# Single-head products in 64-by-32 tiles of the matrix engine, in a packed attention with gated convolution and experts

## The chip, the cores and the metric

The program runs on one core of one Trainium2 chip. The metric is the device time of one execution in microseconds; the figure for a kernel is the median of several executions.

## What is computed

The reference has eight batches of 576 positions and three stages, all in 32-bit floating point.

```python
# q, k, v: (8 batches, 8 heads, 576, 64); p: (8, 8, 32, 64)
p_packed = softmax(p @ k.T / 8) @ v               # 32 packed rows per head
out = softmax(q @ p_packed.T / 8) @ p_packed      # back to 576 rows
x = heads side by side                            # (8, 576, 512)
gate = sigmoid(causal depthwise convolution of x with conv_w, 5 taps)
y = (gate * (x @ w_val)) @ w_out
logits = y @ w_gate; local = sigmoid(y @ w_local)
# each position takes argmax(logits), or the expert of the one before it where local >= 0.5
out = p[e] * (relu(y @ w1[e]) @ w2[e])
```

## The kernel before

**The order of the work.** The kernel is written as tasks. Each task names its engine, an estimated duration and the buffers it reads and writes; `Plan.run` (line 93) plays the program forward with these estimates and emits the tasks in the order in which they would start, the most urgent first by due times. The products of the expert (`expert`, line 828) have goals spaced over a period of 87 us per batch, and everything else is due by what depends on it. So attention of the next batch is laid between the expert products of this one on the matrix engine (PE). `SETUP` (line 186) lists the first transfers in order; those of k, v, q and the two weight matrices go through the queue of SP, and in later batches the loads go through POOL. Four buffers (`RAW`, line 18) hold k, v and q; three buffers in PSUM (`NPP`, pool `psp`) serve all products but those of the expert, which have two of their own (`NPF`).

**The heads.** The eight heads are two groups `g` of four. A group's four heads stand as two pairs. In `s1` (line 335) the operand `pb` is block-diagonal: two heads' p on 128 rows by 64 columns, with zeros in the other halves, so that one product over 128 rows gives two heads' scores in 64 partitions, and two such products side by side fill 128 partitions. Each is done for two halves of 288 positions, four products for a group. Every 32-bit product shows as two PE instructions in the trace, so a group's `s1` is 8 instructions (line 345), tile 128x64, 288 columns.

**The chain of a batch.** For each group: `s1`; its softmax (maximum on DVE line 350, exponential on ACT line 352, into one shared tile `a1`); `a1T`, five transposes (line 366); `a1v` (line 372), which multiplies the 5 blocks of 128 positions by v for two pairs, 20 instructions of 128x64 tiles with 128 columns (line 380), and on DVE scales and masks the result into a block-diagonal `ppf` (line 385); `ppT`, its transpose (line 409); `s2` (line 414), again 8 instructions (line 425) against q; and `mval` (line 504), which multiplies the packed rows by w_val, 4 instructions with 512 columns (line 510). Then come the second softmax, `xT` (line 515: the mixed values, in tiles of 64 rows by 128 columns, one instruction for each product, line 531), the convolution, `val` (the value product by M and the second softmax), `logits` (line 674: 16 instructions in tiles of 128x32, line 684), `route` and `x2`. In batch 0 the scores are first copied to a fixed tile `s2t` and transposed on PE, the taps of the convolution are spread by `taps` (line 548, ahead of all batches) and `conv0` (line 566) replaces `xT`; single products there are in plain 32 bits. Later batches use three products of split operands (`mm3`, lines 298 to 300), one instruction each.

**The first stretch.** `from_f64` (line 876) turns w_val, conv_w and w_out from 64-bit numbers to 32 bits with ACT and DVE (lines 882 to 895), w_val in two halves. `mval` of group 0 needs the first half alone.

Of the kernel before, what the change touches and what calls it, by code (L numbers as in the profile page):

```python
# [17 lines left out]
NP = 32  # L18
# [40 lines left out]
class Plan:  # L59
# [33 lines left out]
    def run(self):  # L93
# [8 lines left out]
        free = dict.fromkeys(engs, 0.0)  # L102
        lock, dma = 0.0, 0.0
# [13 lines left out]
        while todo:  # L117
# [72 lines left out]
def packed_attention_gated_conv_moe(  # L190
# [49 lines left out]
    a1 = const.tile([128, 640], F32, name="a1")  # L240
    s2t = [const.tile([128, 640], F32, name=f"s2t{i}") for i in range(2)]
# [7 lines left out]
    f = {n: Fixed() for n in ("ident", "mask", "cs", "cw", "ww", "wval", "wout", "a1", "s20", "s21", "lt",  # L249
# [69 lines left out]
    def load(b, kind, g, q):  # L319
        if kind == "p":  # L320
            t = st[b, "p"] = ref(ld, [128, 4, 128], F32, "pb", f"pb{b}", 1)
            x = dma(q, 262144, lambda: q.dma_start(t[:], pbd[b]), w=[t], behind=[] if b else done("load"))
            if not b:
                st["load"] = x
            return
# [6 lines left out]
    def pair(i):  # L332
        return slice(i * 64, i * 64 + 64)

    def s1(b, g):
        pb, kt = st[b, "p"], st[b, "k", g]
        r = st[b, "r1", g] = ref(sm, [128, 4], F32, "s1r", f"s1r_{b}_{g}", 2)
        sc = lambda: two(a1[:, 0:S])
        ps = pst([128, 2, 512], f"s1_{b}_{g}")

        def prod():
            for hf in range(2):
                for i in range(2):
                    n = slice(i * S + hf * HS, i * S + hf * HS + HS)
                    nc.tensor.matmul(ps[pair(i), hf, 0:HS], pb[:, 2 * g + i, pair(i)], kt[:, n],  # L345
                                     start=True, stop=True)

        pe(8 * 125, prod, r=[pb, kt], w=[ps], behind=done("a1T"))
# [4 lines left out]
            ps=True, r=[ps], w=[f["a1"], r])  # L353
# [7 lines left out]
    def a1T(b, g):  # L361
        ps = pst([128, 8, 128], f"a1Tp_{b}_{g}")

        def prod():
            for c in range(NT):
                nc.tensor.transpose(ps[:, c, :], a1[:, c * 128:c * 128 + 128], ident)  # L366

        st["a1T"] = pe(5 * 109, prod, r=[f["a1"], f["ident"]], w=[ps], behind=done("a1v"))
# [3 lines left out]
    def a1v(b, g):  # L372
# [4 lines left out]
        def prod():  # L377
            for c in range(NT):
                for i in range(2):
# [5 lines left out]
        dve(188, lambda: stt(pf[:], ps[:, 0:128], r[:, 3:4], mask, ALU.mult, ALU.mult),  # L385
# [20 lines left out]
    def ppT(b, g):  # L406
        pf = st[b, "pp", g][0]
        ps = pss1(f"ppTp_{b}_{g}")
        pe(110, lambda: nc.tensor.transpose(ps[:, 0:128], pf[:], ident), r=[pf, f["ident"]], w=[ps],
           behind=done((b - 1, "s2"), (b - 1, "mval")))  # L410
        t = st[b, "ppT", g] = ref(wk, [128, 128], F32, "ppT", f"ppT_{b}_{g}", 2)
        act(128, lambda: cp(t[:], ps[:, 0:128], AF.Copy), ps=True, r=[ps], w=[t])

    def s2(b, g):


        t, qt = st[b, "ppT", g], st[b, "q", g]
        sT, sk = s2t[g], f[f"s2{g}"]
        pk = pst([128, 2, 512], f"s2k_{b}_{g}")

        def prod():
            for hf in range(2):
                for i in range(2):
                    n = slice(i * S + hf * HS, i * S + hf * HS + HS)
                    nc.tensor.matmul(pk[pair(i), hf, 0:HS], t[:, pair(i)], qt[:, n], start=True, stop=True)  # L425

        st[b, "s2"] = pe(8 * 125, prod, r=[t, qt], w=[pk], behind=done((b - 1, "a2T")))
        if b:
            softmax2(b, g, pk)
            return  # L430
        act(S, lambda: cp(two(sT[:, 0:S]), halves(pk), AF.Copy), ps=True, r=[pk], w=[sk])
# [6 lines left out]
        pe(5 * 109, turn, r=[sk, f["ident"]], w=[ps])  # L438
# [65 lines left out]
    def mval(b, g):  # L504
        t = st[b, "ppT", g]
        ps = pst([128, 2, 512], f"mv_{b}_{g}")

        def prod():
            for i in range(2):
                nc.tensor.matmul(ps[pair(i), 0, :], t[:, pair(i)], wval[:, 2 * g + i, :], start=True, stop=True)  # L510

        st[b, "mval"] = pe(4 * 250, prod, r=[t, (f["wval"], g)], w=[ps], behind=done((b - 1, "val")))
        st[b, "M", g] = operand(b, f"mh{g}", f"ml{g}", ps, DM, lambda: ps[:, 0, :])
# [34 lines left out]
    def taps():  # L548
# [15 lines left out]
        pe(40 * 112, prod, r=[f["cw"], f["ident"]], w=st["taps"])  # L564
# [311 lines left out]
    def from_f64(n, dst, t, at, ct, gt, r, w, eng="DVE", later=0):  # L876
# [5 lines left out]
        act(n, lambda: cp(dst(), low().bitcast(U32), AF.Copy, scale=2.0 ** -52), r=r[:1], w=r[1:], later=later)  # L882
        act(n, lambda: cp(gt(), high().bitcast(F32), AF.Abs), r=r[:1], w=[rg], later=later)
# [260 lines left out]
```

## Time and profile before

| | |
|---|---|
| median of 3 runs | 743.12 us (741.96 to 743.38) |
| the profiled execution's own time | 742.84 us |
| its span, from the first to the last instruction | 741.2 us |
| PE busy | 709.5 us, 96% |
| DVE, ACT, POOL busy | 427.9, 288.0, 236.5 us |
| granted PE clock, mean over the span | 0.992 |

The chain of waits leads back from the last instruction to whatever released each step. The groups of instructions give the busy time of one line; PE instructions overlap there, so a line's sum is less than its count times its mean. How far one run of instructions holds PE is read from the chain, where each piece ends as the next begins.

### The profile page before, as it was taken

The numbers are of one execution on the slowest core, as the hardware profiler recorded it, in microseconds if no ns is written. First come the engines' busy times: TensorE is split into PE (matmuls) and PEld (weight loads), VectorE is DVE, ScalarE is ACT, GpSimd is POOL, SyncE is SP. The second block draws the span as 40 slices with busy tenths as digits, with TensorE's granted clock in tenths as the row PEclk, the third lists the DMA queues.
The fourth block names the chain that finished last, engine by engine and source line by source line (L and its number), as shares of the span: only waits on it lengthen the run. The fifth ranks groups of instructions, "written<-read, shape, count | busy, mean of one in ns | idle before, by whom it ended". The sixth has DMA issues, their size and how long they took to land.

```text
span 741.2 us, 13948 instructions
## 1 busy us (share of the span) xinstructions
PE 709.5 (96%) x5492; PEld 651.8 (88%) x5492; DVE 427.9 (58%) x872; ACT 288.0 (39%) x556; POOL 236.5 (32%) x250
## 2 busy tenths in 40 slices
PE   4689999999999999999989999899999999999996
PEld 2368889989979978997989979899899999999996
DVE  3983589568786878357852578427773463321310
ACT  2534455334543445423433334434343233322420
POOL 1020432244141334302443134422254035424441
PEclk9899999999999999999999999999999999999999
DMA  8611671376262366234452355424143325243421
GB/s 332 254 46 47 213 245 56 124 262 215 82 188 101 117 245 180 88 141 147 157 164 73 127 181 162 126 57 170 49 134 88 142 82 151 80 148 130 128 91 66
DMA packets 35623, 103.59 MB, mean 140 GB/s; under 512 B 4282, under 2 KB 6770, under 8 KB 32994
## 3 DMA queue, kind: packets, MB, share of 16 engines
q0 software_dynamic: 13952, 58.24, 22.5%
q1 hardware_dynamic: 21314, 44.20, 19.9%
q8 instruction: 45, 0.74, 0.4%
q10 hardware_dynamic: 288, 0.21, 0.1%
q14 instruction: 24, 0.20, 0.1%
HBM read 76.48 MB, written 28.52 MB: 142 GB/s over the span
## 4 chain that ended last, share of the span: by engine, by line
PE 88%; DVE 4%; DMA 4%; ACT 1%; issue 1%; POOL 0%; SPq 0%; ACTq 0%; POOLq 0%; DVEq 0%
PE g L298 18%; PE g L300 17%; PE g L299 17%; PE x L298 5%; PE x L299 5%; PE x L300 5%; PE pp L380 3%; PE s L345 2%; PE s2k L425 2%; PE val L299 2%; PE val L300 2%; PE val L298 2%; DMA codes<-rk 2%; PE xT L531 2%; PE mv L510 2%; PE a1Tp L366 1%
## 5 line engine op out<-in xcount | busy, mean ns | idle before, releaser
L313 POOL TENSOR_TENSOR wlo<-raw,whi 128x512 fp32r<-128x512 f32 x128 | 167.2, 1307 | 282.1 <-ACT whi L311 281.6
L298 PE MATMUL g<-x2h,whi 128*128 128x288 f32 x512 | 153.5, 300 | 6.0 <-DVE hl L845 5.7
L298 PE MATMUL g<-hh,whi 128*128 128x288 f32 x512 | 154.9, 302 | 0.0
L300 PE MATMUL g<-x2h,wlo 128*128 128x288 f32 x512 | 151.5, 296 | 0.0
L299 PE MATMUL g<-x2l,whi 128*128 128x288 f32 x512 | 151.3, 296 | 0.0
L300 PE MATMUL g<-hh,wlo 128*128 128x288 f32 x512 | 150.8, 294 | 0.0
L299 PE MATMUL g<-hl,whi 128*128 128x288 f32 x512 | 150.8, 294 | 0.0
L311 ACT ACTIVATE whi<-raw 128x512 fp32r<-128x512 f32 x128 | 80.3, 627 | 108.3 <-PE g L299 58.5
L845 DVE SCALAR_TENSOR_TENSOR hl<-g,hh 128x288 fp32r<-128x288 f32 x128 | 57.8, 454 | 93.7 <-ACT hh L843 93.2
L298 PEld LDWEIGHTS g<-x2h,whi 128*128 128x128 f32 x512 | 96.8, 189 | 10.7 <-DVE hl L845 7.2
L298 PEld LDWEIGHTS g<-hh,whi 128*128 128x128 f32 x512 | 96.2, 188 | 8.7 <-issue 8.3
L843 ACT ACTIVATE hh<-g 128x288 fp32r<-128x288 f32 x128 | 52.6, 411 | 115.7 <-PE g L300 115.5
L299 PEld LDWEIGHTS g<-x2l,whi 128*128 128x128 f32 x512 | 96.7, 189 | 0.0
L300 PEld LDWEIGHTS g<-x2h,wlo 128*128 128x128 f32 x512 | 96.6, 189 | 0.0
L299 PEld LDWEIGHTS g<-hl,whi 128*128 128x128 f32 x512 | 96.1, 188 | 0.0
L300 PEld LDWEIGHTS g<-hh,wlo 128*128 128x128 f32 x512 | 96.0, 188 | 0.0
L543 DVE SCALAR_TENSOR_TENSOR acc<-xT,cw,acc 128x572 f32<-128x572 f32 (+3 forms) x112 | 84.2, 806 | 5.9 <-ACT acc L539 5.9
L298 PE MATMUL x<-gh,wout_hi 128*128 128x288 f32 x256 | 76.0, 297 | 0.0
L299 PE MATMUL x<-gl,wout_hi 128*128 128x288 f32 x256 | 75.7, 296 | 0.0
L300 PE MATMUL x<-gh,wout_lo 128*128 128x288 f32 x256 | 75.3, 294 | 0.0
L863 DVE TENSOR_TENSOR y<-g,rows 128x288 f32<-128x288 f32 x64 | 29.0, 454 | 63.8 <-PE g L300 63.7
L641 DVE SCALAR_TENSOR_TENSOR x2l<-x,x2h 128x576 fp32r<-128x576 f32 x32 | 24.2, 757 | 68.5 <-ACT x2h L640 68.5
(171 smaller groups left out, 1093.7 us busy)
## 6 DMA issues: line engine op xcount, KB each, us to landing
raw<-in_wE_dram SPq DMA_DIRECT2D x128, 256.0 KB, 2.7
xs<-x2h POOLq DMA_DIRECT2D x8, 1152.0 KB, 4.6
xs<-x2l POOLq DMA_DIRECT2D x8, 1152.0 KB, 7.2
v<-in_v_dram POOLq DMA_DIRECT2D x14, 640.0 KB, 5.3
out_dram<-y POOLq DMA_DIRECT2D x31, 288.0 KB, 3.1
k<-in_kT_dram POOLq DMA_DIRECT2D x14, 576.0 KB, 5.3
q<-in_qT_dram POOLq DMA_DIRECT2D x14, 576.0 KB, 4.7
rows<-rk SPq DMA_DIRECT2D x8, 288.0 KB, 3.7
```

The source lines that it names most:

```text
L298: nc.tensor.matmul(o, lhi, rhi, start=start, stop=False)
L299: nc.tensor.matmul(o, lhi, rlo, start=False, stop=False)
L300: nc.tensor.matmul(o, llo, rhi, start=False, stop=stop)
L311: t = act(n, lambda: cp(hi(), src(), AF.Copy), ps=ps, r=r, w=[h], behind=behind)
L313: pool(n, lambda: nc.gpsimd.tensor_tensor(lo(), src(), f32(hi()), ALU.subtract), r=[*r, h], w=[l])
L345: nc.tensor.matmul(ps[pair(i), hf, 0:HS], pb[:, 2 * g + i, pair(i)], kt[:, n], start=True, stop=True)
L380: nc.tensor.matmul(ps[pair(i), 0:128], t[:, c, pair(i)], vt[:, c * 256 + i * 128:c * 256 + i * 128 + 128], start=(c == 0), stop=(c == NT - 1))
L543: dve(S + 60, lambda i=i, j=j, k=k, d=d, acc=acc: stt(acc[:, d:], x(i)[:, 0:S - d], cw[:, j, k:k + 1], acc[:, d:], ALU.mult, ALU.add), r=[ ...
L641: dve(S, lambda: stt(two(xlo[:, m, :]), halves(ps), 0.5, f32(two(xhi[:, m, :])), ALU.mult, ALU.subtract), r=[ps, (xhi, m)], w=[(xlo, m)])
L843: act(HS, lambda ps=ps, u=u, n=n: cp(hh[:, u, n], ps[:, 0:HS], AF.Relu), ps=True, r=[ps], w=[(hh, (u, hf))], goal=goal, urgent=True)
L845: dve(HS, lambda ps=ps, u=u, n=n: stt(hl[:, u, n], ps[:, 0:HS], 0.0, f32(hh[:, u, n]), ALU.max, ALU.subtract), r=[ps, (hh, (u, hf))], w=[( ...
L863: dve(HS, lambda ps=ps, hf=hf, n=n, y=y: tt(y[:, n], ps[hf][:, 0:HS], st[b, "w"][:, n], ALU.mult), r=[ps[hf], st[b, "w"]], w=[(y, hf)], go ...
```

## The change

Every product of a single head becomes a tile of its own of 64 rows by 32 columns. The two groups stand in the upper and lower 64 partitions (`row(g)`), the four heads of a group in four strips of 32 columns (`col(i)`). `s1`, `s2` and `mval` now do both groups in one task, eight heads in turn, and need no zeros. `a1v` keeps a task for each group, with tiles of 128 rows by 32 columns and 64 moving columns. One new ACT step writes the packed rows of both groups into `ppc`, and one transpose replaces two. The inputs are laid out on the host to fit. With them go new estimates and starting values of the planner, another order of the first transfers, a later place of `taps`, two `a1` tiles, four accumulators where there were five, and an exponential ahead of the program's work.

```diff
-        free = dict.fromkeys(engs, 0.0)
-        lock, dma = 0.0, 0.0
+        free = dict.fromkeys(engs, 900.0)
+        lock, dma = 0.0, 2200.0
...
-                dma = max(t.end, dma) + t.size / 290.0
+                dma = max(t.end, dma) + t.size / (RATE if dma < 25000 else 290.0)
...
+STEP8, STEPV = 30, 27
+TAPS, WARM, RATE, S1B = 'a1v', True, 415.0, [(0, 'xT', 1)]
...
-ACC, WLO, F64 = 5, "POOL", "DVE DVE"
-SETUP = "id k0 p v0 q0 cs cw wv0 k1 v1 wv1 q1 wo0 wo1"
+ACC, WLO, F64 = 4, "POOL", "DVE DVE"
+SETUP = "id k0 k1 p v0 cs cw wv0 v1 q0 wv1 q1 wo0 wo1"
...
-            t = st[b, "p"] = ref(ld, [128, 4, 128], F32, "pb", f"pb{b}", 1)
+            t = st[b, "p"] = ref(ld, [128, 4, NP], F32, "pb", f"pb{b}", 1)
...
+    def heads():
+        return [(i, g) for i in range(4) for g in range(2)]
+    def row(g):
+        return slice(g * 64, g * 64 + 64)
+    def col(i):
+        return slice(i * NP, i * NP + NP)
+    def s1(b):
+        pb, kt = st[b, "p"], [st[b, "k", j] for j in range(2)]
+        ps = [pst([128, 2, 512], f"s1_{b}_{g}") for g in range(2)]
+        def prod():
+            for hf in range(2):
+                for i, g in heads():
+                    n = slice(i % 2 * S + hf * HS, i % 2 * S + hf * HS + HS)
+                    nc.tensor.matmul(ps[g][col(i), hf, 0:HS], pb[row(g), i, :], kt[i // 2][row(g), n],
+                                     start=True, stop=True)
+        pe(STEP8 * 32 + 250, prod, r=[pb, *kt], w=ps, behind=done("a1T") + (done(*S1B) if b == 1 else []))
...
             for c in range(NT):
-                for i in range(2):
-                    nc.tensor.matmul(ps[pair(i), 0:128], t[:, c, pair(i)],
-                                     vt[:, c * 256 + i * 128:c * 256 + i * 128 + 128],
+                for i in range(4):
+                    nc.tensor.matmul(ps[col(i), 0:D], t[:, c, col(i)], vt[:, c * 256 + i * D:c * 256 + i * D + D],
                                      start=(c == 0), stop=(c == NT - 1))
-        st["a1v"] = pe(20 * 62, prod, r=[t, vt], w=[ps], behind=done("xT"))
+        st["a1v"] = pe(40 * STEPV + 250, prod, r=[t, vt], w=[ps], behind=done("xT"))
+        act(D + 90, lambda: cp(pc[:, g, :], ps[:, 0:D], AF.Copy, scale=r[:, 3:4]), ps=True, r=[ps, r], w=[(pc, g)])
...
+    def ppT(b):
+        pc = st[b, "ppc"]
+        pe(110, lambda: nc.tensor.transpose(ps[:, 0:128], pc.t.rearrange("p g d -> p (g d)"), ident),
...
+    def s2(b):
+        pk = [pst([128, 2, 512], f"s2k_{b}_{g}") for g in range(2)]
+                for i, g in heads():
+                    nc.tensor.matmul(pk[g][col(i), hf, 0:HS], t[row(g), col(i)], qt[i // 2][row(g), n],
+                                     start=True, stop=True)
...
+    def mval(b):
+            for i, g in heads():
+                nc.tensor.matmul(ps[col(i), g, :], t[row(g), col(i)], wval[row(g), i, :], start=True, stop=True)
+        st[b, "mval"] = pe(16 * STEP8 * 16 // 9 + 250, prod, r=[t, f["wval"]], w=[ps], behind=done((b - 1, "val")))
...
-        pe(40 * 112, prod, r=[f["cw"], f["ident"]], w=st["taps"])
+        pe(40 * 60, prod, r=[f["cw"], f["ident"]], w=st["taps"], behind=done(TAPS))
...
+        s1(b)
         for g in range(2):
-            s1(b, g)
             a1T(b, g)
             a1v(b, g)
-            ppT(b, g)
-            mval(b, g)
+        ppT(b)
+        mval(b)
+        if not b:
+            taps()
...
+        s2(b)
+        for g in range(2):
             a2T(b, g)
...
+    if WARM:
+        cp(lt[64:, 4, :], lt[64:, 4, :], AF.Exp)
```

## Rows read from the trace of the kernel before

**Rows 1.** The page, part 1: busy us of each engine, share of the span, instructions.

```profile
PE 709.5 (96%) x5492; PEld 651.8 (88%) x5492; DVE 427.9 (58%) x872; ACT 288.0 (39%) x556; POOL 236.5 (32%) x250
```

**Rows 2.** The page, part 4: the chain that ended last, by engine.

```profile
PE 88%; DVE 4%; DMA 4%; ACT 1%; issue 1%; POOL 0%; SPq 0%; ACTq 0%; POOLq 0%; DVEq 0%
```

**Rows 3.** Windows: stretch, length, busy us of PE PEld DVE ACT POOL, clock, DMA, GB/s.

```profile
0.00:20.00 20.00, 8.72 (x51) 5.27 (x52) 7.85 (x21) 6.31 (x12) 4.09 (x11) 1.00 0.88 340
20.00:40.00 20.00, 13.65 (x107) 8.28 (x107) 18.91 (x30) 10.62 (x14) 1.60 (x3) 0.83 0.58 219
40.00:65.00 25.00, 23.43 (x157) 19.00 (x157) 17.88 (x24) 11.07 (x16) 4.68 (x2) 1.00 0.06 21
```

**Rows 4.** Groups of PE instructions by line and shape, the lines that the change touches.

```profile
L380 PE MATMUL pp<-v,a1T 128*64 128x128 f32 x320 | 21.9, 286 | 0.8 <-ACT a1T L370 0.8
L345 PE MATMUL s<-k,pb 128*64 128x288 f32 x128 | 20.2, 439 | 5.7 <-DMA pb<-in_pbd_dram 5.7
L425 PE MATMUL s2k<-q,ppT 128*64 128x288 f32 x128 | 19.8, 432 | 1.0 <-ACT ppT L412 1.0
L510 PE MATMUL mv<-wval,ppT 128*64 128x512 f32 x64 | 17.4, 624 | 0.8 <-DVE wval L895 0.6 <-DVE rr L732 0.2
```

**Rows 5.** The chain in order of time: start us, us, engine, tile, line, instructions.

```profile
58.54 3.88 PE val L614 x16
...
62.42 3.47 PE wwp L667 x32
...
154.35 1.09 PE pp L380 x20
155.45 0.86 PE mv L510 x4
156.30 0.97 PE s L345 x8
...
166.63 0.98 PE xT L531 x12
167.61 1.12 PE s L345 x8
```

**Rows 6.** The chain in the window 199 to 202 us, in order of time.

```profile
199.11 1.11 PE lg L684 x16
200.22 1.24 PE pp L380 x20
201.46 0.26 PE ppTp L409
201.72 0.14 PE g L298
```

**Rows 7.** Instructions in order of time, first stretch: start us, us, engine, line.

```profile
5.74 2.19 PE L345 MATMUL s<-k,pb 128*64 128x288 f32 x8 [5.74 <-DMA pb<-in_pbd_dram]
...
7.96 0.76 DVE L350 TENSOR_REDUCE s1r<-s 128x1 f32<-128x576 f32 x1 [6.44 <-PE s L345]
...
8.99 1.28 ACT L352 ACT_TABLE_LOAD   x1 [8.99 <-DVE s1r L351]
...
22.77 2.38 PE L560 MATMUL taps<-ident,cw 128*64 128x128 f32 x40
...
29.19 1.22 DVE L895 SCALAR_TENSOR_TENSOR wval<-gt,wval 128x1024 f32<-128x1024 f32 x1
...
30.72 0.48 PE L409 MATMUL ppTp<-ident,ppf 128*128 128x128 f32 x1 [4.48 <-DVE ppf L385]
...
31.85 2.19 PE L425 MATMUL s2k<-q,ppT 128*64 128x288 f32 x8 [0.65 <-ACT ppT L412]
```

**Rows 8.** DMA issues by line: transfers, count, KB each, median us from issue to landing.

```profile
k<-in_kT_dram SPq DMA_DIRECT2D x2, 576.0 KB, 9.7
...
pb<-in_pbd_dram SPq DMA_DIRECT2D x1, 256.0 KB, 4.3
```

**Rows 9.** The page, part 5: an expert product, its busy us and the idle time before it.

```profile
L298 PE MATMUL g<-x2h,whi 128*128 128x288 f32 x512 | 153.5, 300 | 6.0 <-DVE hl L845 5.7
```

More of the change, by code (lines that the diff above doesn't have):

```diff
@@ L239, in packed_attention_gated_conv_moe @@
     wout_lo = const.tile([128, 4, DM], F32R, name="wout_lo")
-    a1 = const.tile([128, 640], F32, name="a1")
-    s2t = [const.tile([128, 640], F32, name=f"s2t{i}") for i in range(2)]
+    a1 = [const.tile([128, 640], F32, name=f"a1_{i}") for i in range(2)]
     lt = const.tile([128, NT, 9], F32, name="lt")
@@ L320, in load @@
         if kind == "p":
-            t = st[b, "p"] = ref(ld, [128, 4, 128], F32, "pb", f"pb{b}", 1)
-            x = dma(q, 262144, lambda: q.dma_start(t[:], pbd[b]), w=[t], behind=[] if b else done("load"))
+            t = st[b, "p"] = ref(ld, [128, 4, NP], F32, "pb", f"pb{b}", 1)
+            x = dma(q, 65536, lambda: q.dma_start(t[:], pbd[b]), w=[t], behind=[] if b else done("load"))
             if not b:
@@ L365, in prod @@
             for c in range(NT):
-                nc.tensor.transpose(ps[:, c, :], a1[:, c * 128:c * 128 + 128], ident)
-        st["a1T"] = pe(5 * 109, prod, r=[f["a1"], f["ident"]], w=[ps], behind=done("a1v"))
+                nc.tensor.transpose(ps[:, c, :], a1[g][:, c * 128:c * 128 + 128], ident)
+        st["a1T"] = pe(5 * 109, prod, r=[f[f"a1{g}"], f["ident"]], w=[ps], behind=done("a1v"))
         t = st[b, "a1T", g] = ref(wk, [128, NT, 128], F32, "a1T", f"a1T_{b}_{g}", 1)
@@ L404, in operand, with softmax2_0 @@
         return hi, lo
[L406 to L411, printed above, removed]
+    def ppT(b):
+        pc = st[b, "ppc"]
+        ps = pss1(f"ppTp_{b}")
+        pe(110, lambda: nc.tensor.transpose(ps[:, 0:128], pc.t.rearrange("p g d -> p (g d)"), ident),
+           r=[pc, f["ident"]], w=[ps], behind=done((b - 1, "s2"), (b - 1, "mval")))
+        t = st[b, "ppT"] = ref(wk, [128, 128], F32, "ppT", f"ppT_{b}", 2)
         act(128, lambda: cp(t[:], ps[:, 0:128], AF.Copy), ps=True, r=[ps], w=[t])
[L414 to L419, printed above, removed]
+    def s2(b):
+        t, qt = st[b, "ppT"], [st[b, "q", j] for j in range(2)]
+        pk = [pst([128, 2, 512], f"s2k_{b}_{g}") for g in range(2)]
         def prod():
             for hf in range(2):
[L423 to L431, printed above, removed]
+                for i, g in heads():
+                    n = slice(i % 2 * S + hf * HS, i % 2 * S + hf * HS + HS)
+                    nc.tensor.matmul(pk[g][col(i), hf, 0:HS], t[row(g), col(i)], qt[i // 2][row(g), n],
+                                     start=True, stop=True)
+        st[b, "s2"] = pe(STEP8 * 32 + 250, prod, r=[t, *qt], w=pk, behind=done((b - 1, "a2T")))
+        for g in range(2):
+            (softmax2 if b else softmax2_0)(b, g, pk[g])
+    def softmax2_0(b, g, pk):
+        sT = ref(big, [128, 640], F32, f"a2l{g}", f"s2t_{g}", 1)
+        act(S, lambda: cp(two(sT[:, 0:S]), halves(pk), AF.Copy), ps=True, r=[pk], w=[(sT, 0)])
+        dve(64, lambda: nc.vector.memset(sT[:, S:], 0.0), w=[(sT, 1)])
         ps = pst([128, 8, 128], f"s2_{b}_{g}")
@@ L501, in a2T @@
         st[b, "a2T", g] = operand(b, f"a2h{g}", f"a2l{g}", ps, S, lambda: ps[:, 0:S])
-    def mval(b, g):
-        t = st[b, "ppT", g]
-        ps = pst([128, 2, 512], f"mv_{b}_{g}")
+    def mval(b):
+        t = st[b, "ppT"]
+        ps = pst([128, 2, 512], f"mv_{b}")
         def prod():
[L509 to L513, printed above, removed]
+            for i, g in heads():
+                nc.tensor.matmul(ps[col(i), g, :], t[row(g), col(i)], wval[row(g), i, :], start=True, stop=True)
+        st[b, "mval"] = pe(16 * STEP8 * 16 // 9 + 250, prod, r=[t, f["wval"]], w=[ps], behind=done((b - 1, "val")))
+        for g in range(2):
+            st[b, "M", g] = operand(b, f"mh{g}", f"ml{g}", ps, DM, lambda g=g: ps[:, g, :])
     def xT(b, g):
@@ L973, in attention @@
                 load(b, "q", g, nc.gpsimd)
-            s2(b, g)
+        s2(b)
+        for g in range(2):
             a2T(b, g)
@@ L989, in attention @@
         x2_out(b)
-    for t in (a1, *s2t):
+    for t in a1:
         nc.vector.memset(t[:, S:], 0.0)
     nc.vector.memset(lt[64:, 4, :], 0.0)
+    if WARM:
+        cp(lt[64:, 4, :], lt[64:, 4, :], AF.Exp)
+        nc.vector.memset(lt[64:, 4, :], 0.0)
     nc.vector.memset(ww[:, :, 9:], 0.0)
@@ L996, in packed_attention_gated_conv_moe @@
         setup()
-        taps()
         for b in range(B):
```

50 lines of the change are left out of this document (21 added, 29 removed).

## The prediction, made before the change was run

> **What bounds the kernel now.** I read the busy shares first: PE is busy for 709.5 of 741.2 us, DVE for 427.9, ACT for 288.0 [rows 1]. A busy share proves nothing alone, so the chain of waits came next: PE instructions make 88% of what led to the last instruction, DVE and DMA 4% each [rows 2]. The reader is to see that a microsecond taken from PE's own work in the steady part should come off the end. The windows then show where this does not hold: PE is busy for 8.72 of the first 20 us, 13.65 of the next 20, and 23.43 of the 25 after that, while DVE has 18.91 of the second 20 [rows 3]. So there is a head of some 40 us paced by loads and by DVE, and behind it a stretch bound by PE. In the latter the idle time is small: the largest entry before an expert product is 6.0 us in all [rows 9].
>
> The lines that change are large enough to matter: 21.9, 20.2, 19.8 and 17.4 us of busy PE time, 79.3 together [rows 4]. How long each holds PE is better read from the chain, since neighbouring instructions overlap in the busy sums.
>
> **How a tile's price follows from the chain.** One 32-bit product instruction of 288 columns costs 3.88/16 = 0.242 us where its tile is the whole array (`val` of batch 0), 0.97/8 = 0.121 where two tiles of 64 columns take turns (`s`) [rows 5], and 1.11/16 = 0.069 where four tiles of 32 columns do (`lg`) [rows 6]. A share of the last is entry and exit: `s` takes 0.97 beside work of its own kind and 1.12 between other shapes [rows 5], a difference of 0.15 us. Without it `lg` costs 0.96/16 = 0.060. So 0.242, 0.121, 0.060: tiles side by side run together. Tiles above each other do so too: 12 single-pass products of 64 rows in `xT` take 0.98 us [rows 5], 0.082 each, where the expert's whole-array products come every 0.14 [rows 6]. The change combines both, eight tiles. No row shows that combination. The two halvings give 0.030 us an instruction; the bound on the dear side is the 0.060 of `lg`, if only four run together. I take 0.030, since each of the two ways of sharing is shown by itself.
>
> **The change, part by part, for each of batches 1 to 7.** Before, `s` holds PE 0.97 to 1.12 for a group; I count one of each, 2.09 us for two groups.
> - `s1`: 32 instructions at 0.030 = 0.96, with one entry 1.11. Saved: 0.98.
> - `s2`: the same shapes and counts, with about the same busy sum (19.8 us against 20.2 [rows 4]), so 0.98 again.
> - `mval`: 0.86 for 4 instructions of 512 columns [rows 5], 1.72 for two groups. Two tiles give 0.215 an instruction, eight a quarter, 0.054; 16 of them are 0.86. It follows products in the same tiles, or pays one entry of 0.15. Saved: 0.71 to 0.86; I take 0.80.
> - `ppT`: one transpose for two, each 0.26 with its change of shape [rows 6]. Saved: 0.20, a little less since one that stands beside other transposes pays no entry.
> - `a1v`: before, 1.09 to 1.24 for a group [rows 5, 6], so 1.09/20 = 0.054 an instruction. Afterwards there are 40 instructions of half the columns, in four tiles rather than two. By the streams alone they would cost 0.054/4 = 0.0135 each, 0.54 for the group. But each has a load of weights of its own. `wwp`, with 9 columns to stream and 128 to load, takes 3.47/32 = 0.108 an instruction [rows 5]: there the loads set the pace, 0.027 for 32 columns. 40 at 0.027 are 1.08, as much as now. I take that: no gain. The cheap end is 0.0135, a gain of 0.54 for each group; the dear end is the closest spacing that this trace sustains for short products, 0.054 [rows 5], a loss of 1.08 for each group.
>
> Sum: 0.98 + 0.98 + 0.80 + 0.20 = 2.96 us a batch, 20.7 over seven batches.
>
> On other engines: two ACT copies for `ppc` a batch, under 0.3 us each by their 64 columns, hidden beside expert products, with ACT at 39% [rows 1]; if that cover were gone they would cost at most 0.6 us a batch, through the transpose behind them. `s1` and `s2` each hold two of the three PSUM buffers at once, so a following `val` or `x2` has to wait; the cover is the expert's products, which have two buffers of their own. What is late next is the expert stream itself, if it runs dry. Four accumulators instead of five cost nothing as far as four are live in a batch and the next batch's come a period later. p's load falls from 256 KB to 64, on a DMA that no steady wait names.
>
> **The head (batch 0).** Against it: the first products now wait for both halves of k and p, 1216 KB instead of 832 [rows 8], and at 340 GB/s [rows 3] that is 1.2 us later. SP's queue is in order, and q0 now needs k0's buffer, so wv1, q1 and both halves of w_out are issued behind the end of `s1`; `s2` waits for q1. `mval` needs both halves of w_val, the second of which is ready at 30.41 us [rows 7]; its only user is `val`, which starts later. For it: the table load of 1.28 us on ACT [rows 7] moves under the first transfers, both maxima fall into a time when DVE has nothing to do (7.85 busy of the first 20 us), and the second group no longer goes through its own late `ppT` and `s2`. Those now start at 30.72, after PE has stood 4.48 us for DVE, and at 31.85 [rows 7], the latter taking 2.19 us, twice its usual time, in a stretch with a mean clock of 0.83 [rows 3], part of it thus at 1.2 GHz instead of 2.4. `taps`, 2.38 us [rows 7], moves behind `mval`, to a time when PE waits for DVE anyway; without that cover it costs its 2.38. DVE keeps the 18.91 us of 20 that it has, so most of the gain is capped. PE's idle time between 20 and 40 us is 6.35 us. I take a gain of 3, with ends of 3 lost (later loads and uncovered taps, 1.2 + 2.4, less the table load's 1.28) and 7 gained.
>
> **Sum.** 20.7 + 3 = 23.7 us. The profiled execution's time is 742.84, 1.6 over its span, and 0.3 below the median of the runs; from it 719.1. I say **719**.
>
> **The rivals.**
> 1. *The value products gain as well.* If loads into different column strips run together, 14 groups gain 0.54: 7.5 more, 711 us; with the full 7 in the head, 707. For it: `lg` already fits four loads into one round of four products. Against: there the products last long enough to hide four loads of 0.027. The Trainium skill, "TensorE: Matmul & The Clock Gate", section "Measured speedup vs the span model", gives a packed group as one product's time plus some 4 ns for each further tile; it would make this case the forecast, and no row here shows loads under products this short.
> 2. *Eight tiles do not run together*, the change not doing what it says: at 0.060, `s1` is 32 x 0.060 + 0.15 = 2.07 against 2.09, and `mval` 16 x 0.107 = 1.72 likewise. Only `ppT` (1.4 in seven batches) and the head's 3 stay: 738. Against it: `xT` and `lg`.
> 3. *PE cannot take instructions that fast*, the side on which the kernel is slower. The change sends 32 + 32 + 16 + 80 = 160 products a batch through PE where there were 64; if each costs a floor p, they take 160p and some 0.6 for entries. Before it was 2.09 + 2.09 + 1.72 + 2.33 and 0.20 for the second transpose, 8.43 us. The two meet at p = 0.049. The densest sustained spacing here is 0.054 (`pp` [rows 5]); at that, 9.24 us, 0.8 lost a batch, 5.7 in seven, and with no gain in the head 749. For it: nothing denser is sustained anywhere. Against: each dense stretch has another reason (loads or columns) for its pace. The Trainium skill, the same page, section "Wait — 56ns, not 53.3ns?", says that without hardware decoding a matmul takes some 62 ns to decode; by that, an estimate, the batch would take 10.5 us, the whole 758. The 0.054 of `pp` is below it, so the trace speaks against that rule here.
> 4. *The held PSUM buffers or a shifted order stall PE*. Before, stalls ahead of one expert product were 6.0 us [rows 9]. With both groups at once the second buffer waits for the first group's maximum, 0.76 us [rows 7], and, an estimate, as long again for its exponential: 1.5 us in each of seven batches, some 10 us if all of it reached PE: 729. For it: three buffers serve every product but the expert's. Against: the expert's products go on meanwhile.
>
> **How the numbers follow.** Forecast 0.50, first rival 0.23, second 0.09, third 0.07, fourth 0.11. The forecast's own ends, with a head between 3 lost and 7 gained, are 715 and 725. The range reaches from the first rival's 707 to past the fourth's 729, 707 to 733; it leaves out the second and third cases and little else. Some 0.2% is what a measurement of this kernel can tell from no change, 1.5 us. Faster by more: the forecast, the first, the fourth and most of the second, 0.90; within it 0.03; slower 0.07.
>
> **What would show it.** Right: `s` and `s2k` as pieces of about 1.1 us with 32 instructions on the chain, `mv` of 0.85 to 1.0 with 16, one `ppTp` a batch, `pp` still 1.1 to 1.25 with 40; PE's busy time some 20 us lower and still over 95%. Wrong: pieces of `s` near 2 us (second rival), `pp` near 2.2 (third) or 0.7 (first), or more idle time before expert products than 6.0 us (fourth). The head is right if PE's idle time in the first 40 us, 17.63 now [rows 3], is about 3 us less.

## The result and the profile after

| | before | changed |
|---|---|---|
| median | 741.96 us (5 runs, 738.29 to 743.38) | 722.03 us (5 runs, 721.42 to 727.72) |
| the profiled execution's own time, and its span | 742.84, 741.2 us | 727.72, 726.0 us |
| PE busy | 709.5 us | 687.0 us |
| PE idle in the first 40 us | 17.63 us | 22.03 us |
| granted PE clock, mean over the span | 0.992 | 0.977 |

The ratio is 0.9754, with an interval of 0.9728 to 0.978. The kernel is 20 us faster; 719 us was forecast. The profiled execution is the slowest of the five: the other four have spans of 719.2 to 720.5 us at clocks of 0.986 to 0.992. Its rows are read with that in mind.

First the page of the changed kernel, busy us of each engine and then the chain by engine; they answer to [rows 1, 2].

```profile
PE 687.0 (95%) x6124; PEld 640.6 (88%) x6124; DVE 430.7 (59%) x874; ACT 289.8 (40%) x565; POOL 236.1 (33%) x250
...
PE 81%; DMA 8%; DVE 4%; issue 3%; POOL 1%; ACT 1%; SPq 0%; POOLq 0%; DVEq 0%; ACTq 0%
```

PE is busy for 22.5 us less with 632 instructions more. DMA's share of the chain has doubled. The groups of the changed lines (busy us, mean ns of one | idle time before, releaser) answer to [rows 4, 9]:

```profile
L299 PE MATMUL g<-x2h,whi 128*128 128x288 f32 x512 | 154.5, 302 | 3.9 <-DVE hl L866 3.8
...
L391 PE MATMUL pp<-v,a1T 128*32 128x64 f32 x640 | 13.2, 232 | 2.8 <-ACT a1T L381 2.8
L350 PE MATMUL s<-k,pb 64*32 64x288 f32 x256 | 12.4, 478 | 7.4 <-DMA pb<-in_pbd_dram 7.4
L552 PE MATMUL xT<-a2h,pph 64*128 64x288 f32 x56 | 11.1, 352 | 3.9 <-ACT a2h L312 2.7 <-ACT a L363 1.2
...
L440 PE MATMUL s2k<-q,ppT 64*32 64x288 f32 x256 | 10.4, 435 | 2.1 <-ACT ppT L429 2.1
L530 PE MATMUL mv<-wval,ppT 64*32 64x512 f32 x128 | 9.5, 647 | 0.0
```

The four changed lines took 79.3 us and take 45.5. A new idle time of 3.9 us stands before `xT`, where there was none. The chain in order of time (start us, us, tile, line, instructions) answers to [rows 5, 6]:

```profile
66.89 2.10 PE s L350 x32
69.00 2.12 PE lg L705 x16
...
89.55 0.70 PE pp L391 x40
...
101.49 1.13 PE s2k L440 x32
102.62 0.86 PE mv L530 x16
...
106.86 1.13 PE s L350 x32
...
350.88 0.56 PE pp L391 x40
```

Both groups' scores now take 1.13 us where one group took 0.97 to 1.12, `mv` takes 0.86 for both groups, and `pp` 0.56 to 0.70. Near 67 us `s` and `lg` take twice their time: PE's clock is at half there (1.2 GHz). The windows answer to [rows 3]; one behind them is added:

```profile
0.00:20.00 20.00, 6.16 (x86) 3.78 (x90) 11.58 (x30) 8.97 (x15) 3.68 (x10) 1.00 0.90 355
20.00:40.00 20.00, 11.81 (x147) 8.71 (x148) 19.21 (x29) 8.84 (x14) 1.59 (x3) 0.78 0.46 181
40.00:65.00 25.00, 25.00 (x156) 19.43 (x154) 13.12 (x14) 9.90 (x14) 5.21 (x2) 0.91 0.00 1
65.00:100.00 35.00, 34.23 (x328) 30.40 (x328) 12.18 (x42) 12.88 (x31) 11.45 (x14) 0.85 0.53 173
```

In the head PE idles 4.4 us more than before, and the clock falls to 0.78 and 0.85 in two windows. The 1.00 of the first 20 us is not a full clock: the trace's first entry of the clock, at full, stands at 24.2 us (at 16.2 before), and ahead of it the 32 instructions of `s` take 2.17 us, where they take 1.13 later. And the head itself, in order of time (it answers to [rows 7]):

```profile
7.36 2.17 PE L350 MATMUL s<-k,pb 64*32 64x288 f32 x32 [7.36 <-DMA pb<-in_pbd_dram]
...
25.99 1.14 ACT L903 ACTIVATE wo<-out 128x1024 f32<-128x1024 uint32 x1 [2.59 <-DMA out<-in_w_out_dram]
...
27.04 0.25 ACT L429 ACTIVATE ppT<-ppTp 128x128 f32<-128x128 f32 x1
...
27.34 1.98 PE L440 MATMUL s2k<-q,ppT 64*32 64x288 f32 x32 [2.06 <-ACT ppT L429]
...
28.75 2.48 DVE L915 TENSOR_TENSOR wo<-wo,val 128x1024 f32<-128x1024 f32 x2
...
38.42 2.37 PE L518 MATMUL a2Tp<-ident,a 128*128 128x128 f32 x10 [6.13 <-DVE a L477]
```

ACT's copy `ppT` stands behind a conversion of w_out that waits 2.59 us for its data. DVE lays 2.48 us of w_out's conversion ahead of the second softmax, and PE stands 6.13 us for that softmax.

**Where the time went.** If each PE instruction is charged from its start to the next one's start, the profiled executions divide at the first product `x` of batch 0. It starts at 68.65 us before and at 71.84 after, 3.2 later. From there to PE's last instruction it was 666.2 us and is 647.5, 18.8 less before rounding; with idle time counted by itself that splits as follows (us; batches 1 to 7, for `s` 2 to 7, since batch 1's stands ahead of the first `x` in both).

```
s -5.5   s2k -7.25   mv -5.8   pp -7.4   ppT -1.1           taken away 27.1
PE idle +3.3   x +1.6   xT +1.5   expert +1.5   a1T +1.05   given back 9.0
lg, rp, val, rt together -0.7                              net 8.3
```

The 3.2 us ahead of the first `x` arise late. The router's products `wwp` start at 62.26 us before and at 62.51 after, so up to there the two heads are level. Behind that point `wwp`, `s` and `lg` take 2.8 us more, most of it at half clock, and PE waits 0.77 us; five transposes of `a1T`, 0.67 us, no longer stand there. In order of time, the kernel before:

```profile
62.26 3.64 PE L667 MATMUL wwp<-g,woT 128*128 128x9 f32 x32
...
66.42 1.19 PE L345 MATMUL s<-k,pb 128*64 128x288 f32 x8
67.54 1.18 PE L684 MATMUL lg<-acc,ww 128*32 128x288 f32 x16
```

and the changed one:

```profile
62.51 4.39 PE L688 MATMUL wwp<-g,woT 128*128 128x9 f32 x32
...
71.84 0.61 PE L299 MATMUL x<-gh,wout_hi 128*128 128x288 f32 x1 [0.77 <-ACT ltT L710]
```

### The profile page after: what moved, and what is told of

Same layout as the page of the kernel before. It is cut to its first block, busy times and chain, and to the rows that moved or that the text cites. A ratio compares the mean times of both kernels' runs of the same rounds, so it can differ in the third digit from the quotient of the medians.

```text
span 726.0 us, 15236 instructions
## 1 busy us (share of the span) xinstructions
PE 687.0 (95%) x6124; PEld 640.6 (88%) x6124; DVE 430.7 (59%) x874; ACT 289.8 (40%) x565; POOL 236.1 (33%) x250
## 4 chain that ended last, share of the span: by engine, by line
PE 81%; DMA 8%; DVE 4%; issue 3%; POOL 1%; ACT 1%; SPq 0%; POOLq 0%; DVEq 0%; ACTq 0%
PE g L299 17%; PE g L301 16%; PE g L300 15%; DMA codes<-rk 5%; PE x L299 5%; PE x L300 5%; PE x L301 5%; PE val L299 2%; PE val L300 2%; PE val L301 2%; DMA out<-in_w_out_dram 2%; PE xT L552 2%; PE xT L610 2%; PE lg L705 1%; DVE codes L815 1%
## 5 line engine op out<-in xcount | busy, mean ns | idle before, releaser
L299 PEld LDWEIGHTS g<-x2h,whi 128*128 128x128 f32 x512 | 96.7, 189 | 10.2 <-DVE hl L866 5.3
L662 DVE SCALAR_TENSOR_TENSOR x2l<-x,x2h 128x576 fp32r<-128x576 f32 x32 | 24.2, 756 | 62.7 <-ACT x2h L661 62.7
```

What stands on the lines that cost most here:

```text
L299: nc.tensor.matmul(o, lhi, rhi, start=start, stop=False)
L662: dve(S, lambda: stt(two(xlo[:, m, :]), halves(ps), 0.5, f32(two(xhi[:, m, :])), ALU.mult, ALU.subtract), r=[ps, (xhi, m)], w=[(xlo, m)])
```

## The experiments

The kernel before ran beside each group of experiments (1 to 4, 5 to 8, 9 to 11, and 12), with medians of 739.05 to 741.93 us over 11 to 13 runs. Ratios are to it. The changed kernel came out at 722.03 us in the result and at 725.03 in experiment 1 (ratios 0.9754 and 0.9769), and it did not run beside experiments 5 to 12; differences of some 3 us from it are not told apart there.

**1. The changed kernel again**, unaltered.

> The changed kernel once more, unaltered. In its profile TensorE is at 1.2 GHz from 65 to 75 us, just after the router's short products, and loses some 5 us there. If that is a matter of the draw, this run's time is near 722 us, its mean clock 0.985 to 0.992, and the logits of batch 0 take 1.1 us instead of 2.1. If it belongs to the new order of work, it comes back and the profiled time is near 727 us.

Measured: 725.03 us (722.09 to 727.23), ratio 0.9769, interval 0.9726 to 0.9812. The half clock near 65 us came back in its profile:

```profile
66.66 2.10 PE s L350 x32
68.76 2.12 PE lg L705 x16
```

So that stretch is no accident of one execution. It stands in 8 of the 10 profiles of the changed kernel and its variants that leave the router's products as they were, and not in the one of the kernel before.

**2. Value products as before**: tiles of 128x64 with 128 columns; the packed rows come from the masked halves, added on DVE. All else is the changed kernel.

```diff
-                for i in range(4):
-                    nc.tensor.matmul(ps[col(i), 0:D], t[:, c, col(i)], vt[:, c * 256 + i * D:c * 256 + i * D + D],
+                for i in range(2):
+                    m = slice(i * 64, i * 64 + 64)
+                    nc.tensor.matmul(ps[m, 0:128], t[:, c, m], vt[:, c * 256 + i * 128:c * 256 + i * 128 + 128],
                                      start=(c == 0), stop=(c == NT - 1))
...
+        dve(D, lambda: tt(pc[:, g, :], pf[:, 0:D], pf[:, D:2 * D], ALU.add), sb=2, r=[pf], w=[(pc, g)])
```

> The value products go back to tiles of 64 columns with 128 moving columns (20 instructions a group), the rest stays new; the packed rows for the transpose are then summed from the masked halves on DVE. Theory: the value products gained 0.55 us a group, so pieces of 1.1 to 1.25 us come back and the time rises by 14 to 16 times 0.55, 8 to 9 us, to about 730 us. Rival: that gain lies beside other work, and the time stays within 2 us of the changed kernel's.

Measured: 732.83 us (730.3 to 736.43), ratio 0.9871, interval 0.9836 to 0.9906; 7.8 us over experiment 1, which ran beside it. The pieces are those of before:

```profile
87.61 1.24 PE pp L392 x20
```

From first `x` to the end, `pp` took 17.4 us here and 9.6 in experiment 1, again 7.8. The medians differ by as much, with some 3 us of scatter on either, so the value products' gain is real and no loss of it is seen.

**3. The eight heads group after group**, so that the upper and lower rows of the array no longer take turns in the order of issue.

```diff
-        return [(i, g) for i in range(4) for g in range(2)]
+        return [(i, g) for g in range(2) for i in range(4)]
```

> The eight heads go group after group (four heads of the lower 64 rows, then four of the upper) instead of in turn; counts, shapes and plan are the same. Theory: instructions start in order, so only the four strips of one group run together: 0.060 us an instruction as in the logits, s and s2k near 2.0 us and mv near 1.7 for a batch, 2.8 us more in each of eight batches, about 744 us. Rival: the engine looks past them and runs both groups together anyway, and nothing moves: 722 us, pieces of 1.1 us.

Measured: 724.4 us (723.67 to 729.52), ratio 0.9792, interval 0.9746 to 0.9838; no different from experiment 1. `s2k` and `mv` are unmoved:

```profile
99.48 1.13 PE s2k L440 x32
100.61 0.86 PE mv L530 x16
```

The theory that the two groups must take turns falls. Four tiles of one half of the rows and then four of the other go as fast: in either order eight instructions of `s2k` start 5 to 8 ns apart, and the next eight about 0.24 us after the first, which is what one instruction in the whole array costs (0.242 [rows 5]).

**4. Value products head by head**: the same 40 instructions, but five products, ten instructions, in a row in one strip of 32 columns.

```diff
-            for c in range(NT):
-                for i in range(4):
+            for i in range(4):
+                for c in range(NT):
```

> The value products go head by head (five blocks of one strip in a row) instead of strip by strip in turn; counts and shapes are the same. Theory: what pays is that neighbouring instructions stand in different strips; in a row they share a strip and take 0.054 us each, pp near 2.2 us instead of 0.56 to 0.7, some 1.5 us in each of 16 groups, about 746 us. Rival: loads of weights set the pace at 0.027 us, pp near 1.2, about 731 us. Second rival: order is of no account, 722 us.

Measured: 739.35 us (median of 10: 734.64 to 742.67, and one of 1135.94), ratio 0.9963, interval 0.9932 to 0.9993. The pieces fell between what the two sides expected, 2.2 and 1.2 us:

```profile
89.01 1.77 PE pp L391 x40
...
166.98 1.65 PE pp L391 x40
```

So it is turn-taking between strips that makes `pp` cheap: the same work costs 1.65 to 1.77 in this order and 0.56 to 0.70 in the other, 1.07 more for a group. For 14 groups that is 15.0 us; the medians differ by 14.3. The starts in the trace show why the theory's 2.2 us was not reached: 17 of the 39 steps of the group at 89 us are 55 or 56 ns, the 0.054 us that it named, but in three stretches, one for each change of strip, the steps are mostly 25 to 31 ns, as if two strips ran side by side there.

**5. The head: the planner's assumed rate of the first transfers at 340**, near the 340 and 355 GB/s that the windows show, in place of 415.

```diff
-TAPS, WARM, RATE, S1B = 'a1v', True, 415.0, [(0, 'xT', 1)]
+TAPS, WARM, RATE, S1B = 'a1v', True, 340.0, [(0, 'xT', 1)]
```

> Only the planner's rate for the first transfers goes from 415 to 340, about the rate that the first 20 us show; ACT then has both exponentials ahead of the first conversion of w_val, and the copy of the transposed packed rows ahead of the second conversion of w_out. Theory: in the changed kernel ACT, which works in order, stood for w_val and later for w_out with the attention's step queued behind. Then the first transposes start about 1.2 us earlier, s2k about 1.5 to 2 us earlier (27.3 us now), the first x product 2 to 3 us earlier, and the time is 2 to 3 us below the changed kernel's in the same call. Rival: DVE's 19 us of 20 set the pace anyway, and the first x product stays within 0.5 us of 71.8 us.

Measured: 722.78 us (721.28 to 725.74), ratio 0.9762, interval 0.9731 to 0.9794. The order on ACT came out as meant, and PE gained little by it up to `a2Tp`:

```profile
24.15 1.21 PE L440 MATMUL s2k<-q,ppT 64*32 64x288 f32 x32 [0.37 <-ACT ppT L429]
...
26.90 1.31 DVE L908 SCALAR_TENSOR_TENSOR val<-out,val 128x1024 int32<-128x1024 int32 x1
...
29.04 2.48 DVE L915 TENSOR_TENSOR wo<-wo,val 128x1024 f32<-128x1024 f32 x2
...
31.44 1.55 DVE L467 TENSOR_REDUCE s2r<-s 128x20 f32<-128x640 f32 x2
...
38.06 2.37 PE L518 MATMUL a2Tp<-ident,a 128*128 128x128 f32 x10 [8.05 <-DVE a L477]
```

`s2k` starts 3.2 us sooner than in the changed kernel, and `a2Tp` 0.4. PE's wait before `a2Tp` grew from 6.13 to 8.05 us: DVE has w_out's conversion from 26.9 to 31.5, ahead of the softmax. The router's products start 1.0 us sooner (61.47). The first `x` starts at 68.11, 3.7 sooner, more than the theory's 2 to 3, but most of that has another reason: in this profile no half clock follows the router, and `s` and `lg` take 1.1 to 1.2 us each again.

**6. Six unused products of 512 columns in PE's idle time before `a2T` of batch 0**; they add work and change no value.

```diff
+    def warm(n):
+        for j in range(n):
+            ps = ref(psf, [128, 512], F32, "f", f"warm{j}", NPF)
+            pe(870, lambda ps=ps: nc.tensor.matmul(ps[:], ident, wval[:, 0, :], start=True, stop=True),
+               r=[f["ident"], f["wval"]], w=[ps])
...
         s2(b)
+        if not b:
+            warm(6)
```

> Six products of 512 columns whose results nothing uses are added for TensorE, one ahead of and five behind the transposes of batch 0's scores, where it stood idle from 32.3 to 38.4 us. Theory: the idle time costs twice, as the clock falls to 1.2 GHz in it and the products behind (the second transposes, the first half of the convolution) take twice their time to 44.7 us; with the fillers that stretch stays at 2.4 GHz, a2Tp goes from 2.4 to 1.3 us, the first convolution from 7.0 to 5.1, and the time falls by 2 to 3 us. Rival: DVE and ACT behind those products set the pace, and the time stays within 1 us or rises by a late filler.

Measured: 722.1 us (717.13 to 726.68), ratio 0.9754, interval 0.9711 to 0.9797. Of the six runs, two had a clock of 0.998 and took 717.13 and 717.6; the others had 0.985 to 0.991 and took 721.56 to 726.68. The profile is one of the former. Its first `x` starts at 65.61 and no stretch is at half clock before 712 us. The executions at full clock took 4 to 10 us less than the others, but these products do not secure it, and the clock is not all (726.68 was taken at 0.99); the median is that of the changed kernel.

**7. Without the rule that holds batch 1's `s1` behind `xT` of batch 0** (`S1B=[]`).

> The rule that holds batch 1's scores until the convolution of batch 0 is through is dropped; they then stand ahead of the transposes of batch 0's scores at about 31 us. Theory: two microseconds of real work move from 67 us, where they ran at 1.2 GHz ahead of the first x product, into a time of idle TensorE, and the first x product comes about 2 us earlier. Rival: they delay the transposes on which DVE waits by 1 to 2 us, and what is gained at 67 us is lost at 31.

Measured: 727.94 us (724.45 to 728.92), ratio 0.9807, interval 0.9776 to 0.9838. The first `x` came at 75.44 us, 3.6 later than in the changed kernel. The rule is not what makes the head late; without it the head is later still.

**8. Experiments 5 and 6 together.**

> Both edits, the rate of 340 and the six unused products. Theory: the two losses are apart from each other, so the gains add: 4 to 6 us below the changed kernel, about 717 us. Rival: both only move the same wait on DVE, and the pair is no better than the better one.

Measured: 723.38 us (718.5 to 728.32), ratio 0.9756, interval 0.9718 to 0.9795. The two do not add up, and the half clock came at 63.9 us for 6.8.

**9. The router's products with more columns.** `wwp` streams 9 columns; here the same 9 are streamed 14 times, 126 columns, and the first 9 are used.

```diff
-                    nc.tensor.matmul(ps[:, k * 9:k * 9 + 9], woT[:, d * 512 + k * 128:d * 512 + k * 128 + 128],
-                                     g9[:, d, :], start=(d == 0), stop=(d == 3))
+                    nc.tensor.matmul(ps[:, k * 126:k * 126 + 126], woT[:, d * 512 + k * 128:d * 512 + k * 128 + 128],
+                                     g9[:, d, :].unsqueeze(1).to_broadcast([128, 14, 9]),
+                                     start=(d == 0), stop=(d == 3))
```

> The router's 32 products, 9 columns wide, stream the same 9 columns fourteen times over (126 columns, the first 9 used); the loads of 128 weight columns that set their pace of 0.108 us stay. Theory: the clock falls to 1.2 GHz behind this stretch (at 64 to 67 us in six of eight profiles of kernels with the new order) because TensorE loads weights there and multiplies little; with full streams it stays at 2.4 GHz through 75 us, wwp keeps 3.5 us, the logits of batch 0 take 1.1 us instead of 2.1, and the time falls by about 3 us against the changed kernel. Rival: the clock falls from what came before, the idle time up to 38 us, or by the draw, and the same share of runs loses it: no change.

Measured: 724.11 us (721.97 to 725.26), ratio 0.9759, interval 0.9733 to 0.9785. The chain shows the stretch at full clock:

```profile
62.61 3.57 PE wwp L688 x32
...
67.31 1.15 PE lg L706 x16
...
69.19 0.40 PE x L299
```

The half clock near 65 us is gone, at a price of 0.1 us for `wwp` (3.57 where the kernel before took 3.47), and the first `x` starts 2.6 us sooner. The time is no better: 10.2 us at half clock stand at 34.4, as in the changed kernel, and 6.8 at 256.2, behind waits of 1.21 and 0.33 us before `xT`.

**10. w_out's conversion held until the second transposes of batch 0 are through** (and the rate of 340).

```diff
-                     [(v64, 0), (v64, 1), (gt, k)], eng=F64.split()[1], later=LATE)
+                     [(v64, 0), (v64, 1), (gt, k)], eng=F64.split()[1], later=LATE, behind=[st[0, "a2T"]])
...
+        if not b:
+            setup2()
```

> The conversions of w_out are held until the second transposes of batch 0's softmax (with the rate of 340 as well). Theory: in the head DVE works 4.7 us and ACT 2.3 us on w_out between 24 and 34 us, ahead of the softmax that the transposes wait for, and w_out is used 20 us later; held back, the transposes start at 34 to 35 us instead of 38.1 to 38.4, and the first x product moves by as much, to 65 to 68 us; the time falls by 3 us. Rival: w_out's conversions then end so late that the router's transposes or the first x product wait for them, and the gain is given back before 72 us.

Measured: 725.93 us (722.0 to 727.33), ratio 0.9778, interval 0.9748 to 0.9809.

```profile
28.43 1.56 DVE L467 TENSOR_REDUCE s2r<-s 128x20 f32<-128x640 f32 x2 [1.58 <-PE s L456]
...
34.63 2.37 PE L518 MATMUL a2Tp<-ident,a 128*128 128x128 f32 x10 [5.69 <-DVE a L477]
...
70.08 1.62 PE L705 MATMUL lg<-acc,ww 128*32 128x288 f32 x16
```

The softmax starts 3.0 us sooner than in experiment 5, and `a2Tp` 3.4. That shows DVE's order as what paced `a2Tp`. Little of it reaches the rest of the head: the value products of batch 0 start 0.9 us sooner (45.72 for 46.66), since PE waits 0.74 us behind `a2Tp` and does the convolution at half clock until 43.7. The first `x` stands at 66.91, but that is no gain to be read off: in this order `lg`, which stands ahead of `x` in all kernels so far, comes behind its first twelve products. Half clock followed the router again (64.2, 6.8 us) and appeared at 258.8. From first `x` to the end it took 651 us, 3.5 more than in the changed kernel, 1.6 of them `lg`.

**11. Experiments 9 and 10 together.**

> The last two edits together. If both theories hold the gains add, to about 716 us, with the first x product near 64 us and a mean clock of 0.99 or more. If only one holds, the time is that one's; if the loss of the clock is a matter of the draw, neither mean clock nor time differs from the held conversions alone.

Measured: 722.18 us (721.14 to 722.99), ratio 0.9733, interval 0.9709 to 0.9757. First `x` at 66.14 us, again ahead of `lg`, with no half clock behind the router; yet from there to the end it took 648.1 us, with 9.98 us of PE idle time. Two of the stalls, in PE's order of time:

```profile
186.54 0.40 PE L552 MATMUL xT<-a2h,pph 64*128 64x288 f32 x1 [1.47 <-ACT a2h L312]
187.78 0.61 PE L552 MATMUL xT<-a2h,pph 64*128 64x288 f32 x1 [0.84 <-ACT a L363]
...
189.51 0.61 PE L299 MATMUL g<-x2h,whi 128*128 128x288 f32 x1
189.92 0.44 PE L300 MATMUL g<-x2l,whi 128*128 128x288 f32 x1
```

`xT` stands in PE's order before its operand is there; PE waits 1.47 and 0.84 us, and the products behind it run at half clock (0.44 us for one, 0.29 elsewhere).

**12. Experiment 11, and some loads planned later**: v and q of batches 3 and 4 behind the scan of the codes of batches 1 and 2.

```diff
-        st["load"] = dma(q, 512 * n, lambda: q.dma_start(t[:, 0:n], src[b, g]), w=[t], behind=done("load"))
+        st["load"] = dma(q, 512 * n, lambda: q.dma_start(t[:, 0:n], src[b, g]), w=[t],
+                         behind=done("load") + (done(("scan", b - 2)) if b in (3, 4) and kind in "vq" else []))
```

> On top of the held conversions and the wide router, the loads of v and q for batches 3 and 4 are planned behind the scan of the expert codes of batches 1 and 2, instead of right behind the issue of the codes' transfer. Theory: with both groups done at once their buffers come free together, so four loads of 576 to 640 KB follow the codes' transfer within 6 us and slow it (7 to 10 us to landing there, against 4 to 5 in the batches without), DVE waits for the codes in order, and the second softmax behind it leaves TensorE idle near 186 and 255 us, some 5 us of idle time in all with what follows. Then the codes of batches 1 and 2 land in 4.5 to 6 us, that idle time falls to under 2 us, and the time is 2 to 3 us below the 722.2 us of the kernel it is made from. Rival: the transfers of x2 and k ahead of the codes are what slows them, the landing stays above 7 us and the time within 1 us of 722; second rival: v and q come too late and the idle time moves to the value products or s2k.

Measured: 711.64 us (710.45 to 713.12), ratio 0.962, interval 0.9587 to 0.9654: the fastest of all, 10.5 us under experiment 11, or 8 us if both are taken by their ratios. The window from 170 to 270 us, first of experiment 11:

```profile
170.00:270.00 100.00, 94.12 (x837) 87.05 (x834) 71.89 (x146) 44.20 (x87) 33.35 (x38) 0.97 0.48 157
```

and of this one:

```profile
170.00:270.00 100.00, 99.16 (x889) 93.68 (x888) 72.63 (x150) 47.81 (x95) 36.60 (x40) 1.00 0.51 168
```

PE is busy for 99.16 of 100 us at full clock. Behind the first `x` PE idles 4.1 us instead of 9.98, and that stretch takes 638.0 us instead of 648.1: of the 10.1, 5.9 are idle time, 2.05 expert products, 1.8 `xT` and 0.65 `a1T`. The reason that I gave for it is not borne out. The codes took 7.8 and 7.9 us from issue to scan in batches 1 and 2, against 7.2 and 9.8 in experiment 11, one longer and one shorter; in the kernel before they took 9.9 and 12.1, and no wait stands before its `xT`. What the traces do show is the place of `xT`:

```profile
185.99 0.29 PE L301 MATMUL g<-x2h,wlo 128*128 128x288 f32 x1
186.22 0.40 PE L553 MATMUL xT<-a2h,pph 64*128 64x288 f32 x2
186.46 0.29 PE L553 MATMUL xT<-a2l,pph 64*128 64x288 f32 x2
```

Here `xT` starts 13.1 us after the scan of the codes (173.13 us), with expert products up to it and no wait. In experiment 11 PE came to it 10.0 us after the scan (175.09), and waited. It is the first place where the order of PE's work differs between the two: 96 expert instructions stand between `s` and `xT` in experiment 11, and 120 here. An edit of one task can move the planner's order of what follows it. That this order is better is shown; that the loads' own traffic made it so is not. Why the codes land late in some batches stays open, and so does whether the gain needs all three edits, since the last was not run alone.

## Why the prediction was right, and where it was off

**The three lines in eight tiles, and the transpose.** Forecast: 0.98 us a batch for `s1`, 0.98 for `s2`, 0.80 for `mval`, 0.20 for `ppT`. Measured from the two traces: 5.5 us over six batches, and 7.25, 5.8 and 1.1 over seven, or 0.92, 1.04, 0.83 and 0.16 a batch. The seventh `s1`, batch 1's, stands in the head at half clock, 2.10 us instead of 1.13. The two ways of sharing the array do multiply: 32 instructions in 1.13 us, less the entry of 0.15, are 0.031 each, where 0.030 was worked out. The second rival (eight tiles don't run together, pieces near 2 us) and the third (PE can't take instructions that fast, 0.049 or more) are out; no floor of 0.049 us or above for each instruction is seen. No run undoes these three lines, nor the buffers, the order of the transfers or the early exponential; of the products only `a1v` is priced by a run of its own.

**The mis-sized term: `a1v`.** The step that failed is "40 at 0.027 are 1.08, as much as now. I take that: no gain." A group took 0.56 to 0.70. The cheap end, 0.54, was right, and with it the first rival's mechanism: experiment 2 prices it at 7.8 us, and the rival said 7.5. The 0.027 came from `wwp`, whose loads all go into the whole array, one after another. It does not carry over to loads into strips of their own, as experiment 4 shows: where five products in a row share a strip, `pp` costs 1.65 to 1.77, and 0.041 to 0.044 for one. The Trainium skill, "TensorE: Matmul & The Clock Gate", section "Measured speedup vs the span model", has a packed group last as long as one product and some 4 ns more for each further tile; the trace agrees nearly: in `pp` four instructions start 6 to 7 ns apart, and the next four 56 ns after the first, loads included, where 64 columns take some 54 ns by the 0.242 us for 288, an estimate.

**The term of the wrong sign: the head.** "I take a gain of 3" was wrong. In the profiled executions the first `x` came 3.2 us later, which is near the dear end that was named (its own terms, 1.2 + 2.4 - 1.28, make 2.3 and not 3), but by another way. The first product starts 1.6 us later (1.2 was worked out), and PE's idle time in 40 us rose by 4.4; yet by the router, at 62 us, the two heads are level. So what was weighed for and against cancels there, and the gain of 3 is not seen. The other 2.9 us arise behind it, most of them at half clock, for which no step had a price. The sentence "DVE keeps the 18.91 us of 20 that it has, so most of the gain is capped" had the right engine and stopped short of its order. Experiment 5 shows that an earlier `s2k` is lost to DVE, experiment 10 that with w_out's conversion out of the way `a2Tp` moves from 38.06 to 34.63, of which 0.9 us is left at the value products. `taps` was to move behind `mval`; it stands behind `a1v`, ahead of `ppT`, and took 3.90 us where it took 2.38 [rows 7]. That is the clock again: its instructions take 421 ns up to 24 us and 273 behind, where the trace's first entry of full clock stands, and 273 throughout in the kernel before. The kernel before, then the changed one:

```profile
L560 PE MATMUL taps<-ident,cw x40: 272/273/273, 22.8 to 24.9; 128*64 128x128 f32 x40
...
L581 PE MATMUL taps<-ident,cw x40: 272/421/476, 21.1 to 24.7; 128*64 128x128 f32 x40
```

**What the sum left out.** The forecast's parts with the first rival's `pp`, less batch 1's `s`, make 20.7 + 7.5 - 1.0 = 27.2 us; 27.1 were taken away. Of these 8.3 net came back behind the head in the profiled execution, and the sum had no term for that. It is idle time of 3.3 us, work at half clock (10.4 us of it in that stretch, where 3.4 were), and half a microsecond of `a1T`, five of whose transposes were in the head before. The fourth rival, a shifted order that stalls PE, is thus right in kind. Its place is another: not the held PSUM buffers before an expert product, where idle time fell from 6.0 to 3.9, but `xT`, before which it rose from none to 3.9. Experiments 11 and 12 show that this is a matter of order: the same products in another order give 8 to 10 us.

So the 719 came close to 722.03 by luck, by errors against each other: 7.4 us of gain not counted in the steady part, against some 7 in the head (3.2 later, where 3 and batch 1's `s` of 1.0 earlier were forecast) and 8.3 behind it not foreseen, some 8 in all. The profiled execution's 727.72 is 8.6 over the forecast; the other executions, which are nearer, ran at a higher clock (0.986 to 0.992, for 0.977). "PE's busy time some 20 us lower and still over 95%" came out as 22.5 us and 95%, which was not over; "PE's idle time in the first 40 us [...] about 3 us less" came out 4.4 more.

## What to carry to other kernels

Price short products by the strips of the array that they load and stream, not by their count: side by side and above each other they multiply, and in-turn order over column strips is what makes them cheap. When the bounding engine's work shrinks by 27 us, its order was still laid out for the longer work: look for the operation that now stands in the queue before its operand is ready, and expect the order to be worth a good part of the arithmetic (8 to 10 us in experiment 12, which at 711.64 us beats both kernels). In a head that several engines share, the gain of the first step is only as good as the next engine's order.

## What the hardware showed that was not expected

- 20 value products, 40 instructions with 40 loads of weights of their own, run in 0.56 us, 0.014 us from one to the next in the mean. The densest mean spacing that the prediction found in the trace of before was 0.054 [rows 5]. The Trainium skill, "TensorE: Matmul & The Clock Gate", section "Wait — 56ns, not 53.3ns?", states that starts are never closer than about 25 ns; the measurement differs, with starts 6 to 7 ns apart in different column strips.
- Whether tiles in the upper and lower rows take turns makes no difference (1.13 us in both orders), while the same column strip five times in a row costs 1.07 us more for a group of 40 instructions.
- PE's clock fell to 1.2 GHz around the router's 32 products of 9 columns, with no idle time before it, in 8 of 10 profiles of the changed kernel and its variants. With 126 columns in their place it did not in any of three, and the products took 3.57 to 3.78 us against 3.47. In the kernel before, whose router is the same, it did not fall in the one profile, so the products alone don't decide it. What else does is open.
